# A segment-recurrent attention block with its backward pass on one NeuronCore: halved drains, halved softmax steps and a two-part bf16 memory gradient

## Chip, cores and metric

The kernel runs on one core of one Trainium2 chip. The metric is the device time of one launch in microseconds (us): the median of several runs, all outputs included. TensorE is the matrix engine (PE in the profile, its weight loads PEld), VectorE is DVE, ScalarE is ACT, GpSimd is POOL, and SyncE (SP) issues most of the transfers.

## What is computed

The input x has 2048 rows of 512. It is normalised by rows (xn), and the output is x plus an attention branch A(xn) plus a squared-ReLU MLP B(xn). The kernel returns that output and the gradients with respect to x, the first memory and all weights. The attention branch is a recurrence over 64 segments of 32 rows: eight memory rows are put ahead of each segment, and the first eight output rows are the memory of the next segment. With 32 heads of 128:

```python
for s in range(n_seg):
    h = concat([mem, xn[:, 32*s:32*(s+1)]])          # 8 + 32 rows
    q, k, v = h @ Wq, h @ Wk, h @ Wv                 # per head
    p = softmax(where(mask, q @ k.T * scale, -1e9))
    o = (p @ v) @ Wo
    mem, outs = o[:, :8], outs + [o[:, 8:]]
B = relu(xn @ w1 + b1)**2 @ w2 + b2
out = x + concat(outs) + B                           # and jax.vjp of all of it
```

The memory rows may not see the segment's later rows in the way that the segment rows see the memory (the mask), and the backward pass runs the recurrence in reverse: the gradient of a segment's memory rows goes into the output gradient of the segment before it.

## The kernel before, in words

There are four stages, one after the other. **MLP stage** (planner 0): layer norm, MLP forward and backward by blocks of 256 rows. **Forward recurrence** (planner 1): 64 steps, four to a block of 128 rows. **Backward recurrence** (planner 2): 64 steps in reverse. **Weight-gradient stage**: plain loops of 512-column matmuls over the stored gradients (L1650 on).

A step treats 32 rows of all 32 heads at once. These 32 rows are eight memory rows, produced by the step before, and 24 rows of the segment; each segment's own first eight rows ("lead" rows, names with L) do not depend on the memory and are done by blocks beside the recurrence. A tile such as qN has 128 partitions (four head groups of 32 rows) by eight heads by 128. Matmuls come in three shapes: full array (128x128, called "f" in the code), four column groups of 32 (128x32, "w"), and sixteen 32x32 sub-arrays ("d").

**Forward step** (`chain`, L1136). Projections q, k, v (`proj`, L530) accumulate 32 matmuls of 512 columns each in two PSUM banks, one per half of the heads, and each bank is drained by one ACT or DVE instruction (`evict`, L526). `to_T` (L546) transposes four 128x128 blocks per half on TensorE and drains again. The scores go to one bank: a mask matmul (`msk`, L1151, 320 columns) and 32 matmuls of 40 columns. `weights` (L1003) is maximum, subtraction (DVE) and exponential (ACT) over all eight heads; then a copy and two 32x32-block transposes on DVE (L1166 to L1169), `diag` (L614) for the product with v, which drains with a scale (L631: one DVE instruction of 512 columns or four ACT instructions of 128), `sq_T` (L513, DVE transposes), `wo_part` (L1030) for the output projection, and `tm` (L1182) with the copy on L1190 that puts the eight new memory rows into the next step's input. `l_proj`, `l_attn` and the MLP weight gradients (`dw_unit`, L1238: 14 units of 16 pairs of full-array matmuls, operands loaded by SP one block of 128 rows at a time) are filler: work that the recurrence does not wait for.

**Backward step** (`chain`, L1454). gO = projection of the output gradient, its transposes gOT, dP (32 matmuls of 40 columns into one bank, L1465), `smax_bwd` (L1350: four DVE instructions of 320 columns that give dS), the products d2 (`blocks`), d1 (`mixed`) and d0 (`diag`), each drained, transposed by `sq_T` and projected by `dh_part` (L1363) into one fp32 bank for dR. Two instructions copy that bank into R_A (fp32, L435 and L433, halves of 256 columns). Then `gm` (L1521) sums R_A over the four head groups: sixteen fp32 matmuls of eight columns against the selector sel8, and L1528 copies the eight rows into the previous step's gradient input gT. `l_pre` and `l_post` (lead rows) and `keys_part` are filler.

**The order of work** in the first three stages is made at build time by a list planner (`_Plan`, L109). Each operation has a cost per engine, and for TensorE a shape. The planner ranks an operation by the longest path to the end plus a number from the table BIAS, and simulates the engines; a change of TensorE shape costs `_TURN`, and a candidate that needs one is set back in rank by `keep`, the third number of PAR. The emitted order is then fixed on each engine; tiles are guarded by semaphores that the framework places, PSUM tiles by bank.

**Between stages.** Gradients and activations are stored to DRAM in scratch tensors (S_...). Besides the stores of a step there are copies from DRAM to DRAM (S_VM, S_KM, S_HNL, S_GOL, S_BL, and S_OL at the end) that regroup rows. At the end of each forward block, `blk_out` (L1214) transposes the mixed input back (four full-array transposes, hN) and stores it; the backward `blk_out` (L1538, gN) does the same with the gradient. At the change to the last stage, HNc is loaded from S_HNA in blocks of 512 KB.

Of the kernel before, what the change touches and what calls it, by code (L numbers as in the profile page):

```python
# [10 lines left out]
PAR = ((0.3, 0.3, 0.0), (0.61, 7.94, 4.04), (0.09, 2.05, 17.32))  # L11
BIAS_0 = None
BIAS_1 = {
    "l_proj": (
        47.2, 6.5, -41.1, 1.2, 0.8, -33.9, -14.2, 11.4, 20.3, -5.1, -5.3, -14.4, 17.4, 1.5, 7, 20.1, 4.7,
        25.3, -22.2, 55.6, -37, 19.3, -97.5, -1.4, 23, -6.1, -29.3, 48.8, 4.1, 4.5, 52.1, -159.3,
    ),
    "blk_in": (
        11.4, -35.6,
    ),  # L20
# [4 lines left out]
    ),  # L25
    "chain": (
# [4 lines left out]
    ),  # L31
    "blk_out": (
        16.8, -102.8, -36.2, -171.6, -10.2, -72.7, -50.6, -74.7, -96.5, 48.6,
    ),
    "l_attn": (
# [16 lines left out]
    ),  # L52
    "l_pre": (
        46.2, 1.1, -8.1, -100.3, 71, -115.1, -66.8, -4.6, 0.3, -83.5, 0.5, -9.3, -80.7, -12.7, -35.4, -15.9,
        26.3, 9.2, -131.2, 6, 10.9, -47, -9.6, -40.9, 6.9, -128.5, -6.9, -9.4, -61.5, 28.5, -31.2, -38.8,
        -146.2,
    ),
    "load": (
        -43.9, 14.3, -32.2, 2.7, 17.6, -33.7, -80.9, -102.8, 27.2, -48.1, 12.4, -79.8, 33.3, -39.3, -48,
        -45.5, -93.3, -170.2, -64.2, -40.6, -31.9, -8.7, -42, -6.3, 6.8, 15.9, 1.3, 13.8, -17.6, -62.2,  # L60
    ),
    "chain": (
# [5 lines left out]
    ),  # L68
    "blk_out": (
        -22.4, 26.1, -106.9, -65.1, -53.3, 31.4, -76.5,  # L70
    ),
    "l_post": (
# [3 lines left out]
    ),  # L76
# [12 lines left out]
_LINE = 128  # L89
_FETCH = 4.2  # L90


class _PE(dict):
    shape = None
    n = 8


def pe(cost, shape, n=8):
    x = _PE(PE=cost)
    x.shape = shape  # L100
    x.n = n
    return x
# [206 lines left out]
def kernel(  # L309
# [59 lines left out]
    JQ = 4  # L369
# [1373 lines left out]
```

## Time and profile before

| quantity | value |
|---|---|
| median of 3 runs | 2802.92 us (2802.28 to 2803.98) |
| span of the profiled execution | 2798.3 us |
| outside the span, against the median | 4.6 us |
| granted TensorE clock, mean | 0.995 |
| MLP stage | 0 to about 230 us |
| forward recurrence | about 230 to 1240 us |
| backward recurrence | about 1240 to 2240 us |
| weight-gradient stage | about 2240 to 2798 us |

The profile gives for each engine the time it was busy, groups instructions by source line, operation and tiles ("ps_gm<-sel,R_A" writes tile ps_gm from sel and R_A), and for each group says how long the engine stood idle just before it and which instruction ended that wait. "x2016" is a count of instructions. A TensorE instruction is listed with its latency, and several overlap, so the rate is read from the distance between starts. In a timeline row the first number is the start, the second the time to the end of the merged row. Some matmul records are missing from the trace (339 of the 448 dw matmuls are there). The other busy shares of the page, for orientation:

```
DVE  5544455555455555565455455555455402232322
ACT  4333444444444444364444444444444300000000
POOL 1111111111111111145555555555555301112210
```

These are tenths of 40 equal slices: DVE is about half busy through both recurrences, POOL is half busy only in the backward one.

### The profile page before, as it was taken

The numbers are of one execution on the slowest core, as the hardware profiler recorded it, in microseconds if no ns is written. First come the engines' busy times: TensorE is split into PE (matmuls) and PEld (weight loads), VectorE is DVE, ScalarE is ACT, GpSimd is POOL, SyncE is SP. The second block draws the span as 40 slices with busy tenths as digits, with TensorE's granted clock in tenths as the row PEclk, the third lists the DMA queues.
The fourth block names the chain that finished last, engine by engine and source line by source line (L and its number), as shares of the span: only waits on it lengthen the run. The fifth ranks groups of instructions, "written<-read, shape, count | busy, mean of one in ns | idle before, by whom it ended". The sixth has DMA issues, their size and how long they took to land.

```text
span 2798.3 us, 125071 instructions
## 1 busy us (share of the span) xinstructions
PE 2664.6 (95%) x54888; PEld 1538.5 (55%) x55072; DVE 1327.3 (47%) x3327; ACT 985.8 (35%) x2012; POOL 824.8 (29%) x2431
## 2 busy tenths in 40 slices
PE   8998999999999999999999999999999899999999
PEld 6664555555555555575555555555555444444444
DVE  5544455555455555565455455555455402232322
ACT  4333444444444444364444444444444300000000
POOL 1111111111111111145555555555555301112210
PEclk9999999999999999999999999999999999999999
DMA  6657656555557566647777676777766698788861
GB/s 211 202 172 205 180 160 175 164 166 163 156 169 186 169 185 175 177 118 178 187 181 187 179 189 179 189 192 190 188 182 177 201 344 273 232 255 270 257 185 42
DMA packets 499792, 530.91 MB, mean 190 GB/s; under 512 B 223845, under 2 KB 325398, under 8 KB 497070
## 3 DMA queue, kind: packets, MB, share of 16 engines
q1 hardware_dynamic: 480254, 463.06, 59.9%
q0 software_dynamic: 15056, 53.56, 5.6%
q8 instruction: 430, 7.05, 1.1%
q10 hardware_dynamic: 3936, 6.29, 0.7%
q14 instruction: 116, 0.95, 0.1%
HBM read 249.77 MB, written 237.52 MB: 174 GB/s over the span
## 4 chain that ended last, share of the span: by engine, by line
PE 45%; DVE 4%; issue 3%; DMA 3%; ACT 1%; POOL 1%; SPq 0%; DVEq 0%; ACTq 0%; POOLq 0%
PE ps_gw L1690 14%; PE ps_dRA L1370 8%; PE ps_gw L1694 5%; PE ps_gO L538 3%; PE ps_dRL L1370 3%; PE ps_d L624 2%; DMA dLN<-S_GNL 2%; PE ps_d L573 1%; PE ps_d L599 1%; PE ps_gOT L429 1%; PE ps_d L588 1%; PE ps_gm L1524 1%; PE ps_gL L538 1%; PE ps_dL L1481 1%; PE ps_dP L1468 1%
## 5 line engine op out<-in xcount | busy, mean ns | idle before, releaser
L1370 PE MATMUL ps_dRA<-WA,dT 128*32 128x512 bf16 x6144 | 377.0, 381 | 5.3 <-issue 2.5
L1690 PE MATMUL ps_gw<-WA,WB 128*128 128x512 bf16 x1505 | 330.6, 379 | 1.6
L1690 PEld LDWEIGHTS <-WB 128*128 128x128 bf16 x1896 | 185.4, 98 | 225.0 <-issue 1.7
L538 PEld LDWEIGHTS <-PA 128*32 128x32 bf16 x8192 | 195.4, 96 | 192.3 <-DVE PA L1190 22.3
L435 ACT CAST dN<-ps_d 128x512 bf16<-128x512 f32 x372 | 207.4, 590 | 184.7 <-PE ps_d L599 112.3
L1370 PEld LDWEIGHTS <-dT 128*32 128x32 bf16 x6144 | 151.8, 96 | 154.2 <-DVE dT L517 17.3
L433 DVE CAST gwo<-ps_gw 128x512 bf16<-128x512 f32 x64 | 40.0, 685 | 399.9 <-PE ps_gw L1690 268.5
L435 ACT CAST gwo<-ps_gw 128x512 bf16<-128x512 f32 x64 | 33.1, 598 | 510.2 <-PE ps_gw L1690 357.3
L517 DVE STREAM_TRANSPOSE dT<-dN 128x256 f32<-128x256 f32 x384 | 165.4, 437 | 72.1 <-ACT dN L435 66.5
L1020 POOL TENSOR_TENSOR P<-P,rsA 128x320 bf16<-128x320 bf16 x64 | 46.2, 722 | 458.8 <-DVE rsA L1015 244.1
L624 PEld LDWEIGHTS <-PB 32*32 32x32 bf16 x8192 | 119.8, 92 | 76.4 <-DVE PB L1168 23.9
L1701 POOL DMA_DIRECT2D out_dram<-gwo x96 | 71.6, 753 | 293.9 <-ACT gwo L435 265.1
L538 PE MATMUL ps_q<-WA,PA 128*32 128x512 bf16 x2048 | 145.2, 382 | 5.5 <-DVE PA L1190 3.7
L1039 PE MATMUL ps_RA<-WB,OT 128*32 128x256 bf16 x4096 | 129.0, 277 | 17.7 <-DVE OT L517 13.6
L538 PE MATMUL ps_k<-WA,PA 128*32 128x512 bf16 x2048 | 144.9, 381 | 0.3 <-DVE PA L1190 0.3
L435 ACT CAST kN<-ps_k 128x512 bf16<-128x512 f32 x125 | 73.4, 587 | 194.1 <-PE ps_k L538 172.2
L538 PE MATMUL ps_v<-WA,PA 128*32 128x512 bf16 x2048 | 140.7, 379 | 0.0
L1039 PEld LDWEIGHTS <-OT 128*32 128x32 bf16 x4096 | 103.9, 98 | 46.2 <-DVE OT L517 32.0
L538 PE MATMUL ps_gO<-WB,PA 128*32 128x512 bf16 x2048 | 126.4, 380 | 1.0 <-DVE PA L1528 1.0
L611 POOL COPY BDL<-bPLL 32x64 bf16<-32x64 bf16 x256 | 60.4, 236 | 218.4 <-PE ps_d L573 210.4
L433 DVE CAST qN<-ps_q 128x512 bf16<-128x512 f32 x62 | 42.9, 692 | 171.5 <-PE ps_q L538 169.5
L1254 PE MATMUL ps_dw<-sx,anT 128*128 128x512 bf16 x339 | 108.2, 384 | 6.6 <-DMA sx<-S_XN 2.8
(315 smaller groups left out, 5300.8 us busy)
## 6 DMA issues: line engine op xcount, KB each, us to landing
S_GN<-dN SPq DMA_DIRECT2D x192, 256.0 KB
WA<-S_GN SPq DMA_DIRECT2D x150, 256.0 KB
S_Q<-qN SPq DMA_DIRECT2D x64, 256.0 KB
S_K<-kN SPq DMA_DIRECT2D x64, 256.0 KB
S_V<-vN SPq DMA_DIRECT2D x64, 256.0 KB
S_ON<-oN SPq DMA_DIRECT2D x64, 256.0 KB
bqN<-S_Q SPq DMA_DIRECT2D x64, 256.0 KB
bkN<-S_K SPq DMA_DIRECT2D x64, 256.0 KB
```

The costliest lines, as they stand in the source:

```text
L433: nc.vector.tensor_copy(out, in_)
L435: nc.scalar.copy(out, in_)
L517: self.plan.add({"DVE": 0.445}, lambda e, half=half: nc.vector.transpose(words(dst, half).rearrange("p (i c r) -> p i c r", i=4, c=2), src ...
L538: nc.tensor.matmul(bk()[32 * j:32 * (j + 1), :], lhsT=win(dc), rhs=Wt(dc, c0), start=(dc == 0), stop=(dc == DC - 1), tile_position=(0, 32 ...
L611: f(q_(dst, j)[:, :, j, 0:c], q_(src_f(), j))
L624: nc.tensor.matmul(bk()[32 * j:32 * j + m, k * P:(k + 1) * P], lhsT=lf(j, i), rhs=rf(j, i), start=(k == 0 and x == 0), stop=(x == n - 1), ...
L1039: nc.tensor.matmul(bk()[32 * c:32 * (c + 1), :], lhsT=sg.rows(OTt, i, j), rhs=Wo[:, JQ * i + j, dh * DH:(dh + 1) * DH], start=(i == 0 and ...
L1254: nc.tensor.matmul(bks[x]()[:], lhsT=anT[x][:, c, :], rhs=sx[z][:], start=(c == 0), stop=(c == TC - 1))
L1370: nc.tensor.matmul(bk()[32 * j:32 * (j + 1), :], lhsT=sg.rows(XT, i, j), rhs=wtf(t, i, j), start=(first and i == 0), stop=(last and i == N ...
L1690: nc.tensor.matmul(bks[n](), lhsT=HNc[:, rc, dc * P:(dc + 1) * P], rhs=gns[y][:, hf * 512:(hf + 1) * 512], start=(y == 0), stop=(y == NRC ...
L1694: nc.tensor.matmul(bks[n](), lhsT=gns[y][:, k * P:(k + 1) * P], rhs=GOc[:, rc, :], start=(y == 0), stop=(y == NRC - 1))
L1701: nc.gpsimd.dma_start(outWs[t][dc * P:(dc + 1) * P, 4 * hf:4 * hf + 4, j, :], wt[:].rearrange("p (i e) -> p i e", i=4))
```

## The change

**Both recurrences and the planner.** A TensorE operation may offer two shapes. The filler transposes (`to_T` with prio 1, the dw transposes) and the dw matmuls get "wf": in shape w a transpose or matmul of 128 columns of weights becomes four of 32. The planner takes the shape that the array already has. PAR and the BIAS tables are replaced: `keep` goes from 4.04 to 42.99 in planner 1 and from 17.32 to 57.11 in planner 2.

**Forward.** The q and k banks and the qT and kT banks are drained by two instructions each, of 256 columns. The scores go to two banks of four heads, the mask matmul covers only the 32 segment columns, and maximum, subtraction, exponential, copy and both transposes are done by halves of four heads. The scaled drain of `diag` is done by halves of 256 columns. P40 is doubled. The lead-row scores take 32 matmuls of 64 columns in place of 64 of 32. The dw operands are loaded two blocks at a time from the POOL queue.

**Backward.** dP goes to two banks, and `smax_bwd` is done by halves (eight DVE instructions of 160 columns). The lead-row dP takes 32 matmuls in place of 64. The sum over groups takes two bf16 parts of R: R_hi is the upper 16 bits of R_A read in place, R_lo the rest, made by two DVE subtractions; 32 bf16 matmuls take the place of the sixteen fp32 ones.

**DRAM layouts.** S_K, S_V, S_ON, S_GN and S_GNL are re-ordered so that later loads read what the copies had regrouped; the DRAM-to-DRAM copies are gone. The two `blk_out` now copy the memory rows together on POOL, transpose them by four matmuls of shape w, and store 32 rows instead of 128; the last stage loads HNc and GOc from x, gradient and these rows in pieces (`mixed_rows`, `lead_rows`).

```diff
 def pe(cost, shape, n=8):
...
-    x.n = n
+    x.n = {k: n * (4 if k == "w" and len(shape) > 1 else 1) for k in shape}
...
-                turn = o.shape not in (None, shape)
+                turn = bool(o.shape) and shape not in o.shape
...
-            seq.append((o, e))
+            seq.append((o, form if form and len(o.shape) > 1 else e))
...
+    SPLIT = ("q", "k")
+    SPLIT_T = ("qT", "kT")
...
+        def evict2(self, out_f, bk, in_f, key, prio, cost, n=2):
+            self.plan.parts[key] = [(key, x) for x in range(n)]
+            for x in range(n):
+                c = slice(512 // n * x, 512 // n * (x + 1))
+                self.plan.add(cost, lambda e, c=c: ev({"DVE": "v", "ACT": "s"}[e], out_f(c), in_f(c)), [bk], [(key, x)], prio)
...
+                if kind == "c" and nm in SPLIT:
+                    self.evict2(lambda c, half=half: dst[1][:, 4 * half:4 * half + 4, :].rearrange("p i e -> p (i e)")[:, c],
+                                bk, lambda c, bk=bk: bk()[:, c], (dst[0], half), prio, {"DVE": 0.425, "ACT": 0.375})
...
+            form = "wf" if prio else "f"
...
+            for h in range(2):
+                x, bk = slice(4 * h, 4 * h + 4), bks[h]
+                A({"DVE": 0.325}, lambda e, x=x, bk=bk: V.tensor_reduce(mx[:, x], bk()[:], axis=AX.X, op=ALU.max), [bk], [("mxA", h)], 0)
+                A({"DVE": 0.335}, lambda e, x=x, bk=bk: V.tensor_tensor(
+                    out=st[:, x], in0=bk()[:], in1=mx[:, x].unsqueeze(2).to_broadcast([P, 4, KA]), op=ALU.subtract),
+                  [bk, ("mxA", h)], [("stA", h)], 0)
+                A({"ACT": 0.365}, lambda e, x=x: nc.scalar.activation(Et[:, x], st[:, x], ACT.Exp, scale=scale), [("stA", h)], [(pk, h)], 0)
...
-                A(pe(0.435, "f", 2), mm, [("sx", z), ("anT", 0, c // HC), ("anT", 1, c // HC)], [bks[0], bks[1]])
+                A(pe(0.435, "wf", 2), mm, [("sx", z), ("anT", 0, c // HC), ("anT", 1, c // HC)], [bks[0], bks[1]])
...
+        R_hi = R_A.bitcast(BF16).rearrange("p (d z) -> p z d", z=2)[:, 1]
+        R_lo = tl("R_lo", [P, D])
...
-                    def gm(e, hf=hf):
-                        for dc in (2 * hf, 2 * hf + 1):
-                            for j in range(JQ):
-                                nc.tensor.matmul(q_(bm(), j)[:, dc, :], lhsT=R_A[:, dc * P + 32 * j:dc * P + 32 * (j + 1)],
-                                                 rhs=sel8[:], start=(dc == 0), stop=True, tile_position=(0, 32 * j),
-                                                 skip_group_check=True)
-                    A(pe(0.31, "w", 16), gm, [("RA", hf)], [bm], 0)
+                    A({"DVE": 0.35}, lambda e, hf=hf: V.tensor_tensor(
+                        out=R_lo[:, 256 * hf:256 * hf + 256], in0=R_A[:, 256 * hf:256 * hf + 256], in1=R_hi[:, 256 * hf:256 * hf + 256],
+                        op=ALU.subtract), [("RA", hf)], [("Rl", hf)], 0)
+                for part_, key in ((R_hi, "RA"), (R_lo[:], "Rl")):
+                    for hf in range(2):
+                        def gm(e, hf=hf, part_=part_, key=key):
+                            for dc in (2 * hf, 2 * hf + 1):
+                                for j in range(JQ):
+                                    nc.tensor.matmul(q_(bm(), j)[:, dc, :], lhsT=part_[:, dc * P + 32 * j:dc * P + 32 * (j + 1)],
+                                                     rhs=sel8b[:], start=(dc == 0 and key == "RA"), stop=True, tile_position=(0, 32 * j),
+                                                     skip_group_check=True)
+                        A(pe(0.065, "w", 8), gm, [(key, hf)], [bm], 0)
```

More of the change, by code (lines that the diff above doesn't have):

```diff
@@ L139, in add @@
         o.users = []
+        R, W = ([y for k in x for y in (k, *self.parts.get(k, ()))] for x in (R, W))
         R, W = ([k.key if isinstance(k, _Bank) and k.key else k for k in x] for x in (R, W))
@@ L551, in tr @@
                     for k in range(4):
-                        transpose_to(bk()[:, k * P:(k + 1) * P], src[:, 4 * half + k, :])
-                self.plan.add(pe(0.222, "f", 4), tr, [skeys[half]], [bk] + [okeys[half]] * (kind == "f"), prio)
+                        transpose_to(bk()[:, k * P:(k + 1) * P], src[:, 4 * half + k, :], form=e)
+                self.plan.add(pe(0.222, form, 4), tr, [skeys[half]], [bk] + [okeys[half]] * (kind == "f"), prio)
+                if not prio and nm in SPLIT_T:
+                    self.evict2(lambda c, half=half, bk=bk: out_f(half, bk, c)[0](), bk, lambda c, half=half, bk=bk: out_f(half, bk, c)[1](), okeys[half], prio, {"DVE": 0.29, "ACT": 0.375})
+                    continue
                 o, i = out_f(half, bk)
@@ L577, in blocks, with mixed @@
                            bk, lambda bk=bk: bk()[:], [(dst[0], half)], prio, EV_F)
-        def mixed(self, nm, pre, terms, rkeys, dst, prio, lift=0.0):
-            bks = [self.bank("d", [P, 512], F32, "ps_" + nm) for _ in range(2)]
-            for half in range(2):
+        def mixed(self, nm, pre, terms, rkeys, dst, prio, lift=0.0, full=False, inter=False, kind=None):
+            bks = [self.bank(kind or "d", [P, 512], F32, "ps_" + nm) for _ in range(2)]
+            for half in ((0, 1) if not inter else ()):
                 bk = bks[half]
@@ L592, in mixed, with mm0 @@
                 bk = bks[half]
+                if inter:
+                    def mm0(e, half=half, bk=bk):
+                        for k in range(4):
+                            for x, (lf, rf) in enumerate(pre):
+                                nc.tensor.matmul(bk()[:, k * P:(k + 1) * P], lhsT=lf(4 * half + k), rhs=rf(4 * half + k),
+                                                 start=(k == 0 and x == 0), stop=False, skip_group_check=True)
+                    self.plan.add(pe(0.22 * len(pre), "f", 4 * len(pre)), mm0, rkeys[0](half), [bk], prio, lift=lift)
                 def mm(e, half=half, bk=bk):
@@ L597, in mm @@
                         for x, (lf, rf) in enumerate(terms):
+                            if full:
+                                nc.tensor.matmul(bk()[:, k * P:(k + 1) * P], lhsT=lf(i), rhs=rf(i),
+                                                 start=False, stop=(x == len(terms) - 1), skip_group_check=True)
+                                continue
                             for j in range(JQ):
@@ L699 @@
+        for i in range(NI):
+            nc.vector.tensor_copy(maskA[:, i, M:KA], mk[:])
         RB = 2 * P
@@ L1462, in chain @@
             sg.to_T_plain("c", "gOT", gN, "gN", gOT, "gOT", 0)
-            bk = sg.bank("c", [P, NI, KA], F32, "ps_dP")
+            bkp = [sg.bank("c", [P, NI // 2, KA], F32, "ps_dP") for _ in range(2)]
             for half in range(2):
```

483 lines of the change are left out of this document (258 added, 225 removed), and 53 rows, old and new, of tables (BIAS_1, BIAS_2).

## The prediction, on record before the result

> **What bounds the kernel now.** I read the page first: busy shares, then the chain that ended last.
>
> ```profile
> PE 2664.6 (95%) x54888; PEld 1538.5 (55%) x55072; DVE 1327.3 (47%) x3327; ACT 985.8 (35%) x2012; POOL 824.8 (29%) x2431
> ...
> PE 45%; DVE 4%; issue 3%; DMA 3%; ACT 1%; POOL 1%; SPq 0%; DVEq 0%; ACTq 0%; POOLq 0%
> ```
>
> TensorE is busy 95% of the span and is also the largest share of the chain. Next the windows view, one row per stage (PE, PEld, DVE, ACT, POOL busy, clock, DMA):
>
> ```profile
> 240.00:1240.00 1000.00, 933.38 (x23816) 566.88 (x23926) 537.39 (x1294) 446.29 (x913) 154.42 (x293) 0.99 0.61 170
> 1250.00:2240.00 990.00, 944.93 (x26527) 561.15 (x26525) 508.42 (x1266) 405.72 (x807) 533.08 (x1894) 1.00 0.72 185
> 2240.00:2798.30 558.30, 550.13 (x2532) 250.08 (x2581) 147.50 (x242) 33.73 (x65) 93.84 (x137) 1.00 0.74 232
> ```
>
> Both recurrences are bound by TensorE: 67 us without a matmul in flight forward, 45 backward. Every other engine is near half. The last stage is full. So what counts is TensorE time, as long as the recurrence itself, step to step, is not longer than TensorE's work in a step. The memory copies that end each step give the step:
>
> ```profile
> L1190 DVE CAST PA<-ps_mem x63: 191/192/193, 249.6 to 1188.9; 128x32 bf16<-128x32 f32 x63
> L1528 DVE CAST PA<-ps_gm x63: 191/192/193, 1259.8 to 2209.3; 128x32 bf16<-128x32 f32 x63
> ...
> 811.38 0.19 DVE L1190 CAST PA<-ps_mem 128x32 bf16<-128x32 f32 x1 [0.44 <-PE ps_mem L1185]
> ...
> 825.44 0.19 DVE L1190 CAST PA<-ps_mem 128x32 bf16<-128x32 f32 x1 [0.33 <-PE ps_mem L1185]
> ```
>
> 62 steps in 939.3 us are 15.15 us forward, in 949.5 us 15.31 us backward. A single forward step with little filler takes 14.06 us, so forward the recurrence is only some 1.1 us below the mean: TensorE time taken away there can be won, but not without end.
>
> **The change, part by part.** The sum starts from the profiled execution: 2798.3 of span and 4.6 around it, the median 2802.9.
>
> *Turns of the array.* A change of matmul shape has a price that the timeline of one backward step shows (start, time, x count):
>
> ```profile
> 1704.10 0.77 PE L1524 MATMUL ps_gm<-sel,R_A 128*32 128x8 f32 x32
> 1704.70 0.61 PE L538 MATMUL ps_gL<-WB,PB 128*32 128x512 bf16 x8
> ...
> 1708.49 0.22 PE L573 MATMUL ps_d<-gON,BDP 128*128 128x128 bf16 x1
> 1708.54 0.22 PE L573 MATMUL ps_d<-gLN,BDL 128*128 128x128 bf16 x1
> 1708.69 0.43 PE L1468 MATMUL ps_dP<-bVT,gOT 128*32 128x40 bf16 x16
> ```
>
> Full-array matmuls start 0.055 us apart; the first of the other shape comes 0.15 after the last: a turn costs 0.095 us. Counted over the timeline's TensorE rows, the forward window (first two rows below: its first and last of 23816 matmuls) has 550 turns. With dw, kLT, qLT, wT in the shape that stands already and hN in w, the same order has 314: 236 fewer, **-22 us**. Backward (the other two rows, 26527 matmuls) the count goes from 600 to 526 (gLT, gN): **-7 us**.
>
> ```profile
> 242.28 0.23 PE L624 MATMUL ps_o<-vN,PB 32*32 32x128 bf16 x4 [2.56 <-DVE PB L1168]
> ...
> 1239.99 0.22 PE L573 MATMUL ps_d<-gON,BDP 128*128 128x128 bf16 x1
> ...
> 1250.04 0.23 PE L624 MATMUL ps_d<-bkN,PB 32*32 32x128 bf16 x4
> ...
> 2238.73 3.40 PE L1599 MATMUL ps_gw<-WB 128*128 128x512 bf16 x15 [0.16 <-issue]
> ```
>
> The dw matmuls themselves cost the same in shape w: the eight gL ones above take from 1704.70 to 1705.18, 0.06 each, eight for two full ones of 0.22. A larger `keep` may cut more turns or hold the recurrence back; the table is unknown territory and I price it at nothing, with the range around it.
>
> *Memory gradient.* The 32 fp32 passes hold the array from 1704.10 to 1704.70, 0.60 us. How fast do short bf16 matmuls of shape w follow each other?
>
> ```profile
> 1241.20 0.38 PE L1468 MATMUL ps_dP<-bVT,gOT 128*32 128x40 bf16 x32
> ...
> L429 PE MATMUL ps_hN<-ident,PA 128*128 128x128 bf16 x64 | 6.4, 221 | 0.3
> L1108 PE MATMUL ps_scL<-KT,qLT 128*32 128x32 bf16 x1024 | 10.7, 181 | 0.0
> L429 PE MATMUL ps_gN<-ident,PA 128*128 128x128 bf16 x64 | 6.3, 221 | 0.0
> L1404 PE MATMUL ps_dPL<-VTL,LT 128*32 128x32 bf16 x512 | 10.9, 180 | 0.8 <-issue 0.7
> ```
>
> 32 of them in 0.38 us less one latency of 0.18: 6.5 ns each. Bounds for a gm matmul are these 6.5 ns and the fp32 pass's 19 ns; I take 8, near the first, since shape and type are its own. 32 x 8 = 0.25, saving 0.35 in 63 steps: **-22 us**. The Trainium skill, "TensorE: Matmul & The Clock Gate", section "Wait — 56ns, not 53.3ns?", gives a floor of about 25 ns between starts however short the matmul; by it gm would take 0.80 us and cost 13 us more than now. The row speaks against it: column groups of 32 started 6.5 ns apart.
>
> But gm now stands behind two subtractions. What leads up to it:
>
> ```profile
> 1703.67 0.37 ACT L435 COPY R_A<-ps_dRA 128x256 f32<-128x256 f32 x1 [3.83 <-issue]
> 1704.08 0.42 DVE L433 COPY R_A<-ps_dRA 128x256 f32<-128x256 f32 x1 [3.76 <-ACT R_A L435]
> 1704.94 0.19 DVE L1528 CAST PA<-ps_gm 128x32 bf16<-128x32 f32 x1 [0.44 <-PE ps_gm L1524]
> ...
> L433 DVE COPY R_A<-ps_dRA 128x256 f32<-128x256 f32 x64 | 27.2, 424 | 171.8 <-ACT R_A L435 163.0 <-DMA S_GN<-dN 8.7
> L1524 PE MATMUL ps_gm<-sel,R_A 128*32 128x8 f32 x2016 | 38.3, 181 | 5.0 <-issue 0.2
> ```
>
> Now the copy comes 0.44 after R_A is whole (1704.50). After, the subtractions (256 fp32 columns each, 0.42 by the nearest row) follow on the same DVE: one beside ACT's or DVE's copy at best, two in a row at worst, then a short matmul and its latency: some 0.4 to 0.8 us later per step. Queued behind them on DVE stand the copy L1528 itself, so gO, and the dT and LT transposes. The cover is dRL, gL and the keys: before, TensorE idled ahead of gm only 5.0 us in all. The exposed part lies between 0 and 63 x 0.8 = 50; I take the low side, **+10 us**.
>
> *Softmax gradient in halves.* Eight DVE instructions of 160 columns for four of 320:
>
> ```profile
> L1354 DVE TENSOR_TENSOR btA<-ps_dP,bP 128x320 f32<-128x320 f32 x64 | 31.3, 490 | 30.2 <-PE ps_dP L1468 29.3 <-DMA LT<-S_VM 0.6
> L1015 DVE RECIPROCAL rsA<-smA 128x8 f32<-128x8 f32 x64 | 12.9, 201 | 5.8 <-DVE smA L1014 0.5
> ```
>
> 8 columns cost 0.20, 320 cost 0.49, so 160 cost 0.34: 2.7 us for 2.0. The first half can start one dP group earlier (0.3 to 0.5), so dS is whole 0.2 to 0.4 later, beside d2 and its projection (16 full-array matmuls at 0.055 and 32 at 0.06: 2.8 us of TensorE): **0**; uncovered it would cost 25.
>
> *Drains and softmax in halves, forward.* The R_A row has a lesson: of two engines that drain one PSUM bank, the second starts when the first ends (163.0 us of waiting for ACT). The new pairs on the q, k, qT, kT banks are of this kind. Whole and half prices:
>
> ```profile
> L435 ACT CAST qN<-ps_q 128x512 bf16<-128x512 f32 x66 | 38.8, 592 | 2.0 <-PE ps_q L538 1.9
> L433 DVE COPY KT<-ps_kT 128x512 bf16<-128x512 bf16 x124 | 47.3, 420 | 0.4 <-PE ps_kT L429 0.4
> L435 ACT CAST eL<-ps_dL 128x256 bf16<-128x256 f32 x127 | 48.3, 380 | 28.9 <-PE ps_dL L1481 20.1 <-DMA dLN<-S_GNL 3.5 <-DMA bqN<-S_Q 2.5
> L639 ACT ACTIVATE oN<-ps_o,rsA 128x128 bf16<-128x128 f32 x164 | 46.9, 369 | 38.1 <-PE ps_o L624 33.1 <-DVE mxL L994 2.7 <-DVE rsA L1015 1.1
> ```
>
> A k half takes 0.38 + 0.42 in a row for 0.59 (+0.2), a kT half about 0.7 for 0.42 (+0.3). Against this the scores' first half starts the softmax about 0.5 earlier, exponential and DVE overlap, and ACT's four scaled pieces of 0.37 become two. Bounds per step -0.9 and +1.0; in sum I take +0.1, **+6 us**. The Trainium skill, "PSUM — Partial Sum Buffer", section "PSUM bank collisions raise a hardware error", says that two engines must not be in one bank and quadrant at once, reads against reads included; the trace's wait agrees, and the halved drains are against the grain of that rule.
>
> *The rest.* hN, the narrower mask and the lead scores (half the matmuls of the rows above, at 7 to 56 ns each): **-7**; gN and lead dP: **-7**. The copies that go are SP's work beside TensorE: 0. The dw loads on POOL are hidden by its 15% load forward. At the change to the last stage HNc comes in pieces of 256 bytes and 1 KB for blocks of 512 KB:
>
> ```profile
> 2240.00:2250.00 10.00, 7.90 (x59) 3.32 (x59) 0.77 (x2) 0.59 (x1) 0.57 (x1) 1.00 0.99 347
> 2250.00:2260.00 10.00, 9.95 (x47) 4.50 (x46) 0.00 (x0) 0.00 (x0) 0.00 (x0) 1.00 1.04 389
> ```
>
> The DMA engines are full there and TensorE still waits 2 us in 10: between 0 and 8, **+4**.
>
> Sum: -22 - 7 - 22 + 10 + 6 - 7 - 7 + 4 = -45. **2802.9 - 45 = 2758 us.**
>
> **Rivals.**
> 1. *The halves shorten the recurrence.* The forward waits are for it:
>
> ```profile
> L1039 PE MATMUL ps_RA<-WB,OT 128*32 128x256 bf16 x4096 | 129.0, 277 | 17.7 <-DVE OT L517 13.6 <-issue 3.0
> L624 PE MATMUL ps_o<-vN,PB 32*32 32x128 bf16 x2048 | 71.1, 218 | 15.8 <-DVE PB L1168 10.2 <-issue 2.2
> ```
>
> If the +10 and +6 vanish and 30 of the 112 idle us go too: 2712. For it: earlier first halves. Against it: drains in a row.
> 2. *Splitting lengthens the recurrence.* Place: the forward step from the k drain to the product with v. Price: each split pays the fixed 0.2 us twice, +0.5 at the drains, +0.5 on DVE between maximum and product (five steps split, 0.1 each), 1.0 per step, all exposed: +63 in place of the +6. That is -45 + 57 = +12: 2815, **slower**. It decides from 0.8 us of exposed delay per step. For it: 14.06 us steps leave little room. Against it: the mean step has 1.1 us of room, and filler.
> 3. *The shapes do not follow.* If the planner finds no w neighbour for the filler, the turns stay: -45 + 29 = -16: 2787. Against it: the counted order already has these neighbours.
> 4. *gm does not get cheaper*, 19 ns a matmul: -45 + 22 = -23: 2780. The skill's 25 ns would make it 2793; no row here shows them.
>
> **How the numbers follow.** Forecast 0.50 (its own range 2735 to 2785), rival 1 0.22, rival 2 0.16, rivals 3 and 4 0.08 and 0.04. The range reaches from below rival 1 to just past rival 2, 2705 to 2818, and leaves out its outer ends, 0.06 on each side. A difference under 0.2% (5.6 us) cannot be told from none in this kernel: the three times spread by 1.7 us. Slower 0.13 of rival 2 and 0.02 of the forecast's upper end; same 0.05; faster 0.80.
>
> **What would show it.** Right: some 300 turns in the forward window, dw as 128*32 matmuls; gm as bf16 in about 0.25 us; step means near 14.7 us forward and 14.9 backward; the second half-drain waiting for the first. Wrong: forward steps above 15.2 us with idle ahead of ps_sc or ps_o (rival 2); TensorE idle ahead of the lo part of gm near 50 us; idle well under 67 and 45 (rival 1); a last stage that starts more than 8 us late.

## The result, and the profile after

The changed kernel takes **3447.08 us** (median of 4 runs, 3437.50 to 3460.47) against 2803.45 for the kernel before in the same comparison: ratio 1.230, 95% interval 1.227 to 1.233. The forecast of 2758 lies on the wrong side of the kernel before.

The page of after, engine shares and the chain by engine:

```profile
PE 2841.9 (82%) x56728; PEld 1619.3 (47%) x56728; DVE 1463.9 (42%) x4448; ACT 1006.5 (29%) x2302; POOL 933.8 (27%) x2572
...
PE 35%; DMA 10%; issue 5%; DVE 2%; SPq 2%; POOL 1%; ACT 0%; another core or an unknown queue 0%; ACTq 0%; POOLq 0%
```

TensorE went from 95% busy to 82%, and in the chain that ended last DMA went from 3% to 10% of the span. The windows by stage (columns as before: PE, PEld, DVE, ACT, POOL busy, clock, DMA share, GB/s), and the copies that end each step:

```profile
240.00:1440.00 1200.00, 988.68 (x25670) 598.79 (x25668) 607.38 (x1974) 485.21 (x1254) 238.30 (x409) 0.95 0.65 132
1440.00:2860.00 1420.00, 1057.88 (x26456) 612.96 (x26454) 580.54 (x1714) 390.56 (x752) 564.08 (x1937) 0.87 0.72 125
2860.00:3458.70 598.70, 571.14 (x2886) 257.95 (x2885) 154.28 (x263) 38.44 (x75) 94.76 (x142) 0.98 0.78 225
...
L1249 DVE CAST PA<-ps_mem x63: 180/191/193, 258.8 to 1396.6; 128x32 bf16<-128x32 f32 x63
...
L1599 DVE CAST PA<-ps_gm x63: 190/191/193, 1469.0 to 2851.1; 128x32 bf16<-128x32 f32 x63
```

A forward step takes 18.35 us for 15.15, a backward step 22.29 for 15.31: 198 and 433 of the 660 us by which the span grew; the ends and the last stage have the other 29. The second thing to see is the last two columns: the DMA engines are as busy as before (0.65 and 0.72 for 0.61 and 0.72), but move 132 and 125 GB/s for 170 and 185. They are busy for longer with each byte. The granted clock falls too (0.95 and 0.87 for 0.99 and 1.00), and with it TensorE's busy share.

Who waits, from the waits views of TensorE and DVE in after (us in total, times, longest):

```profile
PE ps_dP L1534 <- DVE gOT L437: 165.6, 27, 12.1
```

```profile
DVE LT L542 <- DMA dLN<-S_GNL: 268.3, 33, 14.6
```

The timelines of DVE and TensorE in one slow backward step join the two:

```profile
2007.51 0.19 DVE L1599 CAST PA<-ps_gm 128x32 bf16<-128x32 f32 x1 [0.33 <-PE ps_gm L1595]
2014.17 0.77 DVE L542 STREAM_TRANSPOSE LT<-dLN 128x256 f32<-128x256 f32 x2 [6.47 <-DMA dLN<-S_GNL]
2014.87 0.71 DVE L437 COPY gOT<-ps_gOT 128x512 bf16<-128x512 bf16 x2
...
2015.30 0.33 PE L1534 MATMUL ps_dP<-bVT,gOT 128*32 128x40 bf16 x16 [3.78 <-DVE gOT L437]
```

A filler transpose (LT) stands ahead of the recurrence's copy gOT in DVE's queue; DVE is idle for 6.47 us until its load is there, and the recurrence waits behind it. Before, DVE's wait for dLN was 49.1 us in all. So the question is why loads are late. The first place to look is SP, where one transposing load (VR, the segment's v rows of a backward step) shows its price at the issue itself (min/median/max ns), before and after:

```profile
L1377 SPq DMA_TRANSPOSE VR<-S_V x64: 1231/1268/2481, 1218.0 to 2184.3; - x64
```

```profile
L1444 SPq DMA_TRANSPOSE VR<-S_V x64: 1283/3420/6812, 1422.0 to 2828.1; - x64
```

The median issue went from 1.27 to 3.42 us. What the DMA engines do meanwhile, in windows of after (the last two columns are DMA share and GB/s again):

```profile
1666.00:1668.00 2.00, 0.91 (x6) 0.12 (x6) 0.00 (x0) 0.00 (x0) 0.00 (x0) 0.79 0.91 319
1668.50:1670.00 1.50, 1.50 (x17) 1.50 (x16) 0.52 (x2) 0.75 (x2) 0.00 (x0) 0.50 0.27 99
1677.00:1677.50 0.50, 0.50 (x16) 0.28 (x12) 0.50 (x2) 0.00 (x0) 0.42 (x3) 1.00 1.21 156
1679.50:1681.00 1.50, 1.38 (x73) 1.02 (x76) 1.00 (x3) 0.96 (x2) 0.40 (x2) 1.00 0.27 104
1685.00:1687.00 2.00, 2.00 (x56) 1.54 (x52) 1.20 (x4) 1.37 (x4) 0.00 (x1) 1.00 0.26 101
```

The first window holds stores of 128 rows in one dimension (R): 0.91 and 319 GB/s. Three windows have a DMA share of 0.26 to 0.27 at 99 to 104 GB/s (the last two follow a store of S_GN and a load of kN, issued at 1679.02 and 1679.66 us): about four of the sixteen engines work, each at the rate at which sixteen gave 389 GB/s before (the row 2250 to 2260 of the prediction). Counted over the packet records, the commonest number of 2 KB packets in flight at once is 16 before and 4 after. In the window at 1677 us a transpose starts: the share jumps over 1, the rate stays low. Its packets have 256 bytes, and over the whole run 1722 packets of this size take over 1.6 us in after (7450 us of engine time), 134 before (265 us).

**Theory A, narrow transfers.** The new layouts make the stores of S_V, S_K, S_ON and S_GN and the load of kN into accesses whose outermost dimension is four (j, row, 2 KB) where it was 128 (row). Such a transfer goes to four engines. (The Trainium skill, "DMA: Bandwidth & Descriptors", sections "Why a DMA increments its semaphore by 16 and not by 1" and "Rules for kernel authors", says the same: the number of engines is the largest one up to 16 that divides the slowest dimension of both sides, and an outermost dimension of c under 16 confines a transfer to at most c engines. The windows at 0.26 agree.) They fall behind, a transpose that needs all sixteen waits for them and holds the other twelve, and every later load is late. (Narrow transfers are not new: the kernel before has them too, of 64 KB, in the stores S_GNL<-eL, two a step, and the copies S_VM and S_KM. New are those of 256 KB.) **Theory B:** the 8 KB between the rows of S_K and S_V makes the accesses slow. **Theory C:** the new order puts waiting filler ahead of the recurrence. **Theory D:** the dw loads on POOL hold up the transposes.

### The profile page after: what moved, and what is told of

It reads as the page before. It is cut to its first block, busy times and chain, and to the rows that moved or that the text cites. A ratio compares the mean times of both kernels' runs of the same rounds, so it can differ in the third digit from the quotient of the medians.

```text
span 3458.7 us, 130027 instructions
## 1 busy us (share of the span) xinstructions
PE 2841.9 (82%) x56728; PEld 1619.3 (47%) x56728; DVE 1463.9 (42%) x4448; ACT 1006.5 (29%) x2302; POOL 933.8 (27%) x2572
## 4 chain that ended last, share of the span: by engine, by line
PE 35%; DMA 10%; issue 5%; DVE 2%; SPq 2%; POOL 1%; ACT 0%; another core or an unknown queue 0%; ACTq 0%; POOLq 0%
PE ps_gw L1768 12%; DMA dLN<-S_GNL 7%; PE ps_dRA L1437 7%; PE ps_gw L1772 4%; PE ps_gO L569 3%; PE ps_dRL L1437 2%; PE ps_d L675 1%; SPq L504 1%; PE ps_d L612 1%; PE ps_d L649 1%; PE ps_dL L1547 1%; PE ps_gOT L433 1%; DMA V<-S_K 1%; PE ps_dP L1534 1%; PE ps_d L627 0%
## 5 line engine op out<-in xcount | busy, mean ns | idle before, releaser
L1437 PE MATMUL ps_dRA<-WA,dT 128*32 128x512 bf16 x6144 | 408.8, 404 | 12.6 <-issue 12.4
L569 PEld LDWEIGHTS <-PA 128*32 128x32 bf16 x8192 | 223.3, 102 | 247.0 <-issue 102.4
L1534 PE MATMUL ps_dP<-bVT,gOT 128*32 128x40 bf16 x2048 | 40.2, 194 | 189.1 <-DVE gOT L437 165.6
L569 PE MATMUL ps_gO<-WB,PA 128*32 128x512 bf16 x2048 | 153.5, 439 | 37.9 <-issue 33.1
L662 POOL COPY BDP<-bP 32x256 bf16<-32x256 bf16 x256 | 104.1, 407 | 258.8 <-PE ps_d L612 188.3
L1312 PE MATMUL ps_dw<-sx,anT 128*32 128x512 bf16 x1768 | 131.5, 397 | 51.0 <-DMA sx<-in_grad_out_dram 22.5
L1095 PE MATMUL ps_RA<-WB,OT 128*32 128x256 bf16 x4096 | 136.9, 278 | 39.0 <-DVE OT L542 35.5
L542 DVE STREAM_TRANSPOSE LT<-dLN 128x256 f32<-128x256 f32 x96 | 38.6, 428 | 272.2 <-DMA dLN<-S_GNL 268.3
L1437 PE MATMUL ps_dRL<-WA,LT 128*32 128x512 bf16 x1536 | 128.7, 442 | 12.9 <-DVE LT L542 7.3
```

What stands on the lines that cost most here:

```text
L542: self.plan.add({"DVE": 0.445}, lambda e, half=half: nc.vector.transpose(words(dst, half).rearrange("p (i c r) -> p i c r", i=4, c=2), src ...
L569: nc.tensor.matmul(bk()[32 * j:32 * (j + 1), :], lhsT=win(dc), rhs=Wt(dc, c0), start=(dc == 0), stop=(dc == DC - 1), tile_position=(0, 32 ...
L662: f(q_(dst, j)[:, :, j, 0:c], q_(src_f(), j))
L1095: nc.tensor.matmul(bk()[32 * c:32 * (c + 1), :], lhsT=sg.rows(OTt, i, j), rhs=Wo[:, JQ * i + j, dh * DH:(dh + 1) * DH], start=(i == 0 and ...
L1312: nc.tensor.matmul(bks[x]()[m:m + w, :], lhsT=anT[x][:, c, m:m + w], rhs=sx[z][:, c % 2, :], start=(c == 0), stop=(c == TC - 1), tile_posi ...
L1437: nc.tensor.matmul(bk()[32 * j:32 * (j + 1), :], lhsT=sg.rows(XT, i, j), rhs=wtf(t, i, j), start=(first and i == 0), stop=(last and i == N ...
```

## Experiments on the layouts and queues

**e1_cut4: the changed kernel, narrow transfers cut in four.** Addresses and planned order stay.

```diff
-sg.dma(lambda: step_rows(S_V, s), lambda: flat(vN), ...)
+sg.cut(lambda j: (S_V[b][:, j, v], q_(flat(vN), j)), ...)   # 4 x dma_start of 32 rows
 (the same for S_K, kN, S_ON, S_GN)
```

> The changed kernel, with the same addresses, the same operations and the same planned order; only the transfers of S_V, S_K, S_ON and S_GN whose outermost dimension is four (j, r, row) are each issued as four transfers of 32 rows, one for each j. Theory A, narrow transfers: such a transfer moves on four of the sixteen DMA engines (the trace of after shows four packets of 2 KB in flight at a time where before shows sixteen), those four fall behind, and the transposes, which need all sixteen, stop the other twelve. It expects the packets of 256 bytes over 1.6 us gone, 15 to 16 us a step in both recurrences, and 2780 to 2900 us. Theory B, the 8 KB stride between the rows of S_K and S_V: addresses are unchanged, so 3400 us or more. Theory C, the new order (larger keep, new BIAS tables) puts transposes that wait for a load in front of the recurrence on DVE: the order is unchanged, so 3400 or more.

Measured 3135.21 us, ratio 1.118 (1.115 to 1.120). Three rows of it, the transpose and the copies of both stages:

```profile
L1451 SPq DMA_TRANSPOSE VR<-S_V x64: 1252/1282/2828, 1263.5 to 2495.8; - x64
...
L1256 DVE CAST PA<-ps_mem x63: 179/191/193, 252.9 to 1239.5; 128x32 bf16<-128x32 f32 x63
...
L1606 DVE CAST PA<-ps_gm x63: 190/191/193, 1311.4 to 2511.9; 128x32 bf16<-128x32 f32 x63
```

The transposes are back at 1.28 us, 58 long packets (256 bytes, over 1.6 us) are left of 1722, and the forward step is 15.91 us: same rows, same strides, same order. That is against B and C as the main cause. Backward the step stays at 19.36: SP now has 25.8 issues a step for 13.8, 935 us of issuing in 1201, and DVE still waits 214 us for dLN. That the number of issues is the reason is argued; e5_cutkv below, with 16.8 a step, fits it. The expected 2780 to 2900 overlooked this price.

**e2_rv: S_GN and S_ON back in the old layout**, S_K and S_V still narrow.

```diff
-S_GN = dt_([3, TC, JQ, SPB, RA, HW], ...)
+S_GN = dt_([3, TC, P, SPB, HW], ...)      # S_ON alike; HNc, GOc rows in the order (r v)
```

> The changed kernel with S_GN and S_ON in the layout of before (128 rows at a stride of 8 KB, one dimension) and HNc and GOc loaded in the row order that goes with it; S_K and S_V stay as changed. Theory A: three of four narrow transfers of a backward step are gone and one of three of a forward step: backward 22.3 to about 17 us a step, forward 18.35 to about 17, together 2950 to 3150 us. Theory B: the rows of 8 KB stride are more, not fewer: 3440 or more. Theory C: 3400 or more.

Measured 3074.62 us (one run): backward 17.06 us a step (expected 17), forward 17.48. With one transfer of 256 KB that is narrow in a backward step in place of four, most of the loss is gone.

**e3_gn_alone: the kernel before with the new S_GN layout alone.**

```diff
-S_GN = dt_([3, TC, P, SPB, HW], ...)
+S_GN = dt_([3, TC, JQ, SPB, RA, HW], ...)
-sg.dma(lambda: part_of(S_GN[t], s, SPB), ...)
+sg.dma(lambda: S_GN[t, b][:, v], ...)
 (the last stage's loads of these rows follow the layout)
```

> The kernel before with one part of the change alone: S_GN in the changed layout, so that the three stores of each backward step have the outermost dimension four; the last stage reads the same rows in the old order. Theory A: forward unchanged (15.15 us a step), backward from 15.3 to between 18 and 21 us a step, 3000 to 3150 us in all. Theory B: the stride between rows falls from 8 KB to 2 KB, so 2800 or a little less. Theory C: the order is that of before, so 2800 within 1%.

Measured 3014.68 us (one run).

```profile
L1190 DVE CAST PA<-ps_mem x63: 190/192/194, 249.5 to 1186.9; 128x32 bf16<-128x32 f32 x63
...
L1528 DVE CAST PA<-ps_gm x63: 151/192/193, 1259.7 to 2417.5; 128x32 bf16<-128x32 f32 x63
...
L1377 SPq DMA_TRANSPOSE VR<-S_V x64: 1244/2522/4272, 1216.0 to 2387.0; - x64
```

The forward stage is unchanged (15.12 us a step), the backward step goes to 18.67: three narrow stores cost 3.36 us a step, 1.1 us each. The rows of the store moved closer together (2 KB for 8 KB), so B had expected a gain. The VR transpose, which nobody touched, has its median issue doubled to 2.52 us: it is the victim. 1349 packets of 256 bytes take over 1.6 us here. This run shows the cause alone, in an order that was not changed; how the DMA engines hand the delay on, the second half of theory A, is inferred.

**e4_sx_sp: the changed kernel, dw loads issued by SP.**

```diff
-sg.dma(lambda z=z: sx[z][:], ..., lat=3.2, cost=0.62, eng="POOL")
+sg.dma(lambda z=z: sx[z][:], ..., lat=3.2)
```

> The changed kernel with the loads of the dw operands (sx) issued by SP in place of POOL, still two blocks at a time. Theory D, the loads on the POOL queue hold up the transposes anT and so the forward recurrence: forward from 18.35 to under 16.5 us a step, 3330 or less in all. Theories A, B and C: 3420 to 3480.

Measured 3405.19 us (one run): forward 17.23 us a step, backward 22.57 (22.29 in after). The POOL queue has a share, forward (42 us in all), below what D needed; D is not the main cause.

**e5_cutkv: S_GN and S_ON in the old layout, S_K and S_V cut in four** (the edits of e2_rv and, for S_V, S_K and kN, of e1_cut4).

> The changed kernel with S_GN and S_ON as in the run with the old row order, and the transfers of S_K and S_V (8 KB between rows, as changed) issued as four of 32 rows each. No transfer of 256 KB is narrow now. Theory A: both recurrences at 15 to 16 us a step, 2790 to 2880 us; the six further issues a step forward and three backward cost SP time (0.5 us each), less than the twelve that made SP the limit of the backward steps when everything was cut. Theory B, the stride of the rows of S_K and S_V adds to it: packets of 256 bytes stay long and the time stays over 2950.

Measured 2935.17 us (2 runs), ratio 1.046 (1.044 to 1.048): 16.09 us forward, 16.22 backward. Above A's upper end of 2880, but below B's 2950, and only 183 long packets.

**e6_oldkv: all attention scratch in the old layouts.**

```diff
-S_K = dt_([TC, RA, JQ, SPB, HW], ...)
+S_K = dt_([NSEG, P, HW], ...)             # S_V, S_VL alike; copies S_KM, S_VM are back
```

> The changed kernel with every layout of the attention scratch (S_K, S_V, S_VL, S_GN, S_ON, and the copies S_KM and S_VM) as before: what is left of the change is the compute part, the new order and the DMA of dw and of the last stage. If the rest of the change does what was forecast, 2740 to 2780 us, with steps of 14.5 to 15.0 us; if the halves lengthen the recurrence or the new order holds it up, 2800 to 2870, with steps over 15.3.

Measured 2895.85 us, ratio 1.033 (1.029 to 1.037). The scratch layouts cost 551 of the 644 us (512 by e5_cutkv). What is left of the change is still 88 us slower than before, above both expected ranges, and not 45 faster. The DMA engines are back at 180 GB/s with a share of 0.70 (1300 to 2300 us). Forward it takes 16.27 us a step, backward 15.48; its shortest forward step is 14.59 us against 14.00 before.

## Experiments on what is left

**e7_gm_fp32 and e8_drains_whole: parts undone in e6.** The fp32 memory gradient, and whole drains of q, k, qT, kT.

```diff
-for part_, key in ((R_hi, "RA"), (R_lo[:], "Rl")):   # e7: sixteen fp32 matmuls on R_A, sel8
...
-for x in range(n):                                   # e8: one drain of 512 columns
```

> The kernel with the old scratch layouts (e6) and the memory gradient by sixteen fp32 matmuls a half of R instead of two bf16 parts. By the forecast's terms (22 us saved on TensorE, 10 lost behind the subtractions) it is 12 us slower than e6; if the subtractions cost the recurrence 0.4 to 0.8 us a step it is 5 to 30 us faster.

> The kernel with the old scratch layouts (e6) and the q, k, qT and kT banks drained by one instruction each, the softmax still in halves. If two half-drains in a row cost what their durations say (0.2 us for k, 0.3 for kT), it is 10 to 30 us faster than e6, all of it in the forward recurrence; if the halves shorten the recurrence, 10 to 30 us slower.

Measured 3018.38 (ratio 1.075, 1.074 to 1.077) and 2915.43 (1.039, 1.035 to 1.043). (Empty operations keep the places in the tables.) e7 is 123 us above e6, far outside what was expected; e8 is 20 above it. Neither can be trusted as a price: the fp32 sum shortens the shortest backward step (13.56 us for 14.13), yet the mean goes from 15.48 to 17.38. The planner's tables are tied to the operations of the changed kernel; that the broken order makes the difference is argued, not shown. e8's interval overlaps that of e6. So the next runs put one part into the kernel before, **with the order of all its operations kept**.

**p1_gm_alone.**

```diff
 def gm(e, hf=hf):
+    V.tensor_tensor(out=R_lo[:, x], in0=R_A[:, x], in1=R_hi[:, x], op=ALU.subtract)
+    # 8 bf16 matmuls of R_hi of this half; after the second half 16 of R_lo
```

> The kernel before, its order of operations unchanged, with the memory gradient alone changed: in the place of each half's fp32 matmuls stand the subtraction on DVE and the bf16 matmuls of the two parts. By the forecast's terms (TensorE 22 us less, 10 us more behind the subtractions) 12 us faster than before. If TensorE wins nothing and the recurrence gets longer by what its shortest steps show (14.13 us with the two parts, 13.58 with fp32 in the kernels with the old scratch layouts), up to 35 us slower.

Measured 2830.27 us, ratio 1.0085 (1.0063 to 1.0107): 25 us slower. The timelines of DVE and TensorE in one step:

```profile
1702.56 0.42 DVE L433 COPY R_A<-ps_dRA 128x256 f32<-128x256 f32 x1 [2.91 <-ACT R_A L435]
1702.90 0.79 DVE L1527 TENSOR_TENSOR R_lo<-R_A 128x256 bf16<-128x256 f32 x2
1704.02 0.19 DVE L1535 CAST PA<-ps_gm 128x32 bf16<-128x32 f32 x1 [0.33 <-PE ps_gm L1531]
```

```profile
1702.76 0.49 PE L1531 MATMUL ps_gm<-sel8b,R_A 128*32 128x8 bf16 x16
1703.37 0.21 PE L1531 MATMUL ps_gm<-sel8b,R_lo 128*32 128x8 bf16 x8
1703.74 0.21 PE L1531 MATMUL ps_gm<-sel8b,R_lo 128*32 128x8 bf16 x8 [0.16 <-DVE R_lo L1527]
1703.89 0.23 PE L624 MATMUL ps_dqL<-bkLN,dSTLL 32*32 32x128 bf16 x4
```

Each group of matmuls is short, as forecast. But nothing else runs between them: TensorE's queue holds from 1702.76 to 1703.74 while it waits for the two subtractions, and the copy comes 1.26 us after the first matmul, where before it came 0.84 after (1704.10 to 1704.94). Over all 63 steps the medians are 1.44 and 0.84, so the copy comes 0.60 us later; 0.38 us of it shows in the mean step (973.1 us for 949.5 in 62 steps), 24 us in all. That nothing runs between the parts is due to this run, which puts both into one place of the order. The changed kernel plans them apart, and in e6_oldkv other matmuls stand between them in 40 of 63 steps. So 25 us is the price in this order, not in the other.

**p2_drains_alone.**

```diff
+ev("s", o[:, 0:256], i[:, 0:256])
+ev("v", o[:, 256:512], i[:, 256:512])
```

> The kernel before, its order unchanged, with the q, k, qT and kT banks alone drained in two halves, the first by ACT and the second by DVE; scores and softmax stay whole. By the forecast's durations (k +0.2, kT +0.3 us where the halves follow each other) up to 0.5 us a step: 0 to 31 us slower, all of it forward; faster if two engines do drain one bank side by side.

Measured 2810.91 us, ratio 1.0019 (1.0004 to 1.0033). The waits of DVE:

```profile
DVE kN L433 <- ACT kN L435: 148.4, 64, 4.3
```

The DVE half of k waits for the ACT half in each of the 64 steps, as predicted; the mean step is 15.29 us for 15.15. A difference of that size in one profile is not sure: p1_gm_alone, whose forward stage is that of before, has 15.26. The 6 us rest on the medians.

**p3_shapes_alone.** The planner's order of before; a filler transpose or dw matmul is issued in shape w when the array stands in w.

```diff
+now = "w" if o.both and now == "w" else o.shape
```

> The kernel before, its order unchanged, with the shapes alone changed: the filler transposes and the dw matmuls are issued in shape w where the array stands in w. Forecast: 236 turns of the array fewer forward, some 20 fewer backward, at 0.095 us: 22 us faster. If a turn costs nothing where TensorE waits anyway, or w costs more than f, 0 to 8 us faster.

Measured 2817.15 us, ratio 1.0046 (1.0031 to 1.0061). Counted from the first memory copy to the last, turns fell from 532 to 354 in 62 forward steps (8.6 to 5.7 a step) and from 579 to 527 backward. Time did not fall.

```profile
240.00:1240.00 1000.00, 926.62 (x25141) 576.48 (x25189) 535.65 (x1291) 442.73 (x909) 154.03 (x293) 0.99 0.62 170
...
PE ps_dw L1267 <- DMA sx<-S_XN: 8.0, 7, 2.0
```

TensorE is less busy in the window (926.62 for 933.38) and the steps are no shorter (15.23 for 15.15, backward 15.46 for 15.31). Its wait for the loads of sx went from 2.8 to 8.0 us. Why it is 12 us slower, not equal, is open.

**p4_lead_alone.**

```diff
-for c in range(2):                        # lead scores: two matmuls of 32 columns
-    ... rhs=KT[p][:, :, i * JQ + j, M * c:M * c + M]
+... rhs=KT[p][:, :, i * JQ + j, 0:2 * M]  # one of 64; lead dP alike; mask on columns M:KA
```

> The kernel before, its order unchanged, with the lead-row scores and lead-row dP in 32 matmuls of 64 columns in place of 64 of 32, and the mask matmul on the segment columns only. Forecast, without hN and gN, which stay: about 10 us faster (4 for the scores, 5 for dP, 1 for the mask); 0 if this filler only makes room for waiting.

Measured 2793.78 us, ratio 0.9953 (0.9935 to 0.9970): 11 us faster, the one part that gives what was forecast. The place is another: the step is 14.90 us for 15.15 forward, but 15.35 for 15.31 backward, so the 5 us of dP do not show.

**p5_halves_alone.** Softmax and softmax gradient in halves, one bank each as before.

```diff
-V.tensor_tensor(out=st[:], in0=bk()[:], in1=Ptile[:], op=ALU.mult)
+V.tensor_tensor(out=st[:, x], in0=bk()[:, x], in1=Ptile[:, x], op=ALU.mult)   # x: four heads; all steps alike
```

> The kernel before, its order unchanged, with the softmax of a forward step (maximum, subtraction, exponential, copy, two transposes) and the softmax gradient of a backward step alone done by halves of four heads, scores and dP still in one bank each. Forecast: nothing backward, and forward, with the drains, +6 us. If each split pays its fixed time on the recurrence, 0.3 to 0.5 us a step forward: 20 to 30 us slower.

Measured 2839.01 us, ratio 1.0126 (1.0106 to 1.0146): 36 us slower.

```profile
L1560 DVE CAST PA<-ps_gm x63: 191/192/193, 1272.6 to 2253.1; 128x32 bf16<-128x32 f32 x63
...
L1374 DVE TENSOR_TENSOR btA<-ps_dP,bP x4: 311/322/324, 1701.3 to 1718.4; 128x160 f32<-128x160 f32 x4
...
L1380 DVE SCALAR_TENSOR_TENSOR maskA<-btA,bP x4: 325/442/571, 1702.5 to 1719.6; 128x160 bf16<-128x160 f32 x4
```

Backward it is 15.81 us a step (+0.50), forward 15.31 (+0.16, little more than p1's +0.11 without a change there). A half of 160 columns takes 0.32 to 0.44 us where 0.34 was forecast; the cover was wrong, the halves lie on the recurrence. This is likely an upper bound for the change, where dP has two banks and the first half can start earlier.

**t1_before_plain, t2_e6_plain, t3_e6_sx_sp: tables and queue.**

```diff
-BIAS = (BIAS_0, BIAS_1, BIAS_2)
+BIAS = (None, None, None)                 # t1 on before, t2 on e6 with PAR of before; t3: e6 with the edit of e4
```

> The kernel before with its BIAS tables empty: the planner ranks by path length alone. It prices the tables. If the tables are worth little, 2800 to 2830; if they carry much of the order, 2880 or more.

> The changed kernel with the old scratch layouts (e6), with PAR of before and empty BIAS tables. Against the kernel before with empty tables it shows the change without its tables. If the 88 us that e6 stands above before come from the new tables and the larger keep, it stands within 40 us of that kernel; if they come from the halves, the two-part sum and the loads, it stands 70 us or more above it.

> The changed kernel with the old scratch layouts (e6), with the sx loads issued by SP instead of POOL. If the POOL queue delays them as it did in the changed kernel (42 us), 20 to 40 us faster than e6; if that cost came with the narrow transfers, within 10 us of e6.

Measured 3175.05 (ratio 1.131, 1.129 to 1.134), 3149.49 (1.122, 1.120 to 1.125) and 2880.24 (1.028, 1.024 to 1.032). The tables are worth 372 us to the kernel before. Without tables on either side the rest of the change is 26 us faster; with them it is 88 slower. So its sign depends on the order that stands around it. t3 cannot be told from e6.

**b1_lead_copies: a version that beats both.** p4, and the copies S_VM and S_KM turned.

```diff
-mrow(D_[b])[:, M * v:M * (v + 1), :]
+mrow(D_[b])[:, M * v:M * (v + 1), :].rearrange("j m f -> m j f")   # source alike
```

> A version meant to beat both kernels: the kernel before with the lead-row matmuls of the run p4, and with the DRAM-to-DRAM copies S_VM and S_KM, whose outermost dimension is four (j, row), issued in the order (row, j) with an outermost dimension of eight. p4 alone gave a ratio of 0.995. Theory A: the copies hold eight engines instead of four for half as long, so the same or some 5 us less than p4; if the copies hinder nobody, the same as p4, 2785 to 2798.

Measured 2786.65 us, ratio 0.9935 (0.9922 to 0.9949). It beats both kernels. Its interval overlaps that of p4, so what the copies give is not settled.

## Why the prediction was wrong, step by step

**The step that failed: "The copies that go are SP's work beside TensorE: 0."** The layouts were priced by the copies that they save and not by what the stores cost in their new order. 551 of the 644 us stand here, through a chain that no term of the sum had: narrow stores, slow transposes, late loads, DVE's queue, the recurrence. e3_gn_alone shows it alone, e1_cut4 takes 312 us of it away at the same addresses and in the same order, and e2_rv gives 372 us back with fewer narrow transfers. The whole diff has the outermost dimension of four in `step_rows` and in the stores of S_GN, and the prediction passed over it. The DMA share of 0.61 and 0.72 in its own windows showed queues that were far from idle.

**Turns of the array, -22 and -7: did not come.** The number fell, though less than counted (532 to 377 in 62 forward steps of after, 354 in p3), the time did not: +12 us. The 0.095 us holds for more than the row it was read from: backward, a matmul of 512 columns is followed by one of another shape after 0.31 us (median), where full ones in a row start 0.216 apart. What failed is the step from TensorE's time to the kernel's: TensorE is 7 us less busy in p3's forward window, and the steps are no shorter.

**Memory gradient, -22 and +10: wrong sign, +25.** The matmuls are short, but a sum in two parts is done only when the second part is there. "0.4 to 0.8 us later" was right (0.60). That TensorE would win 0.35 beside it was the error, in p1 at least, where the two parts sit in one queue with the wait between them. For the order of the changed kernel the price is open. Rival 4 (not cheaper) came nearer, for another reason.

**Softmax gradient in halves, 0: wrong cover.** "Uncovered it would cost 25": p5 shows 31 backward with one bank. With two banks it is not settled.

**Drains and softmax in halves, +6: right in sign, too small.** +6 for the drains, at most 10 for the softmax (0.16 a step in one profile), inside the bounds of -0.9 to +1.0 a step. **The rest, -14:** -11 of it came in p4, by luck in part: forward alone, where 5 of the 10 were due. hN and gN were not run alone.

**dw loads on POOL, 0:** 42 us in the changed kernel, not measurable in e6. **Last stage, +4:** it begins 28.3 us after the last backward copy for 26.6, but takes 17 us more (579.3 for 562.4), in windows such as these of after:

```profile
2870.00:2880.00 10.00, 8.29 (x175) 3.50 (x163) 2.45 (x6) 3.25 (x7) 0.24 (x2) 0.90 0.56 152
2880.00:2900.00 20.00, 7.35 (x78) 3.04 (x79) 1.23 (x3) 0.00 (x0) 0.29 (x1) 0.66 0.41 129
```

TensorE is idle for 13 of 20 us while DMA moves 129 GB/s. What it waits for is this:

```profile
2892.31 0.29 POOL L1612 COPY maskL<-PA 128x128 bf16<-128x128 bf16 x1 [22.01 <-DMA out_dram<-maskL]
...
2892.65 0.30 PE L1619 MATMUL ps_gN<-ident,maskL 128*32 128x128 bf16 x4 [12.89 <-POOL maskL L1612]
```

The gN transposes wait for a copy on POOL, and POOL for a small store (out_dram<-maskL) to leave the tile. SP issued that store at 2888.15 us, behind loads of HNc in pieces (WB<-S_XN, WB<-S_HM). So the pieces cost their place in SP's queue; the DMA engines were not full.

**Tables and keep, "priced at nothing":** the order is worth hundreds of microseconds (372 in the kernel before), more than any part but the layouts. What the new tables and the larger `keep` cost is not separated: t2 speaks for them as the source of the 88 us that e6 stands above before. The parts alone sum to +68 (25, 12, 6, 36, less 11) of the 88. That is near, but they were measured on the other order, so the split of these 88 stays open.

**Rivals.** Rival 2 had the side and, in e6, its shape: the shortest forward step grew by 0.6 us (14.59 for 14.00), where it priced 1.0. It added 57 us to the sum; most of the real 644 came from elsewhere.

## What to carry to other kernels

Read the access pattern of every transfer that a layout change touches, on both sides, and ask over how many engines its outermost dimension spreads; a saved copy is not the price. In the profile, a DMA share that stays while GB/s falls (0.72 at 125 for 185) was the sign of it. Price a part by putting it alone into the kernel before with the order kept: undoing a part in an order made for it misled here by over 100 us (e7). Even so the price holds for that order only.

## What the runs showed of the hardware

- A 256 KB transfer with an outermost dimension of four moved at about 100 GB/s with a DMA share of 0.26; as four transfers of 32 rows the same addresses did no harm to the transposes (issue 1.28 us).
- A transposing load is slow beside such transfers: in e3_gn_alone its median issue doubled to 2.52 us although its own source was untouched. That it waits for the busy engines and holds the others fits the share of 1.21 at 156 GB/s when one starts, but no run shows it alone.
- With narrow stores alone TensorE has long waits in the backward stage that the profile puts down to "issue", that is, to nothing that it shows. The waits of e3_gn_alone, and the longest of this kind before:

```profile
PE ps_dRA L1370 <- issue: 31.1, 18, 4.4
PE ps_gm L1524 <- issue: 23.9, 13, 3.7
```

```profile
PE ps_dP L1468 <- issue: 6.2, 9, 0.9
```

  Late instructions are a guess: the page lists instruction queues among the DMA queues, but the 16 KB packets of the larger one take no longer (median 1.11 us from 1300 to 2200 us, before 1.08).
- The granted clock went down with TensorE's share of work: 0.87 in the backward stage of after, where TensorE is busy for 1057.88 of 1420 us, and 1.00 before, with 944.93 of 990.
